# Fewer weight tiles decoded beside the attention pairs, one PSUM layout for all stages, and the transposes of the exponentials one pair later

## The chip, the core and the metric

The kernel runs on one core of one Trainium2 chip. The metric is the device time of one execution in microseconds (us), as a median of several runs. A core has a matrix engine (PE, which also loads the stationary operand, PEld), a vector engine (DVE), a scalar engine (ACT), a third elementwise engine (POOL), and a queue that issues DMAs (SP). Each runs its own list of instructions in order; semaphores tie them to each other.

## What is computed

Three blocks follow each other: causal attention with a memory term, a feed-forward block with the gate h * tanh(softplus(h)), and a second block that multiplies two projections.

```python
scores = scale * np.matmul(q, k.transpose(0, 1, 3, 2))      # B, H, S, D = 4, 8, 576, 64
scores = np.where(causal, -1000000000.0, scores)
a = np.exp(scores - scores.max(-1, keepdims=True))
local = np.matmul(a / (a.sum(-1, keepdims=True) + 1e-09), v)
q_p = phi(q)                                                 # x > 0: x + 1, else exp(x)
mem_out = einsum(q_p, M_prev) / (einsum(q_p, z_prev) + 1e-06)
x = g * mem_out + (1 - g) * local                            # 2304 rows, 512 columns
h = x @ w_in                                                 # 512 to 2048
x2 = (h * np.tanh(softplus(h))) @ w_out                      # 2048 to 512
out = ((x2 @ w1) * (x2 @ w2)) @ w3 @ w_out2                  # 512 to 1024, 1024, 512
```

All weights come as 64-bit floats, so the kernel has to make 32-bit words of them itself.

## The kernel before

**Tiles to decode.** A weight tile of 128 rows and 512 columns arrives as 512 KB of pairs of 32-bit words. `decode` (lines 104 to 133) turns it into fp32: six operations on DVE (lines 114, 116, 118, 121, 125 and 127) and one addition on POOL (line 132). `to_split` (lines 149 to 154) then writes two parts, `hi` and `lo`, with two more operations on POOL (lines 77 and 80); `to_dram` does the same and sends the result to DRAM for later. A decoder has a number of raw buffers and of working buffers: beside the attention one of each, in the middle stage three and two.

**The attention** goes over 16 pairs of heads, one turn p of the loop at line 521 for each pair, and a 17th turn, the drain. In a turn PE makes the scores of four row blocks (`s_blocks`) and of the last 64 rows (`s_last`). DVE adds the mask and takes the maximum (line 374), ACT takes the exponential with its sum (line 379), and `normed` (lines 358 to 371) multiplies the exponentials by the inverse sums: DVE takes five blocks, POOL four (line 369 both). PE then transposes the exponentials in seven groups (`pt_g`, lines 422 to 432): group 1 and group 0 hold blocks of the pair's first head, 2 and 3 of the second, 4 blocks of both, 5 and 6 the last rows. ACT copies each group out of its PSUM bank (line 431). `pv` multiplies them by v, after a product of `phi` with the memory matrix; `prep` and `trans_phi` transpose q, k and phi for the next pair, through the two banks called X. `in_turn` ties each of these pieces behind PE's last instruction, so the order of PE is the order of the calls; the rest is put in order by a scheduler.

In turn p groups 4, 2, 3, 5 and 6 of pair p - 1 are transposed among the scores of pair p. Groups 1 and 0 of pair p come at the end of the same turn p, behind `pv` of pair p - 1. A tile is decoded in each of the turns 2 to 11: eight of the first quarter of the weights (`lq0`: four of w_in, four of w_out) and two of those for later (`pre`). The scheduler puts each about a turn earlier.

**The middle stage** has 24 units (g, n): a quarter g of the hidden columns and a chunk n of 384 rows. `emit_h` makes four products h of 128 columns and passes them through tanh, arctan and sine on ACT. DVE multiplies the result `y` by h (line 493); this last reading of h frees its PSUM bank. `split_y` splits the product, `emit_x2` multiplies it by w_out and DVE adds it to x2 (line 610). On PE a unit is 48 matmuls of h and 48 of x2 of the unit before. Two tiles are decoded beside nearly every unit of g = 0 to 2. In g = 3 `fold` multiplies w3 by w_out2 on PE beside the units, 16 tiles of w3.

**PSUM** has eight banks. The attention takes two pairs A, two X and two F. At the end of the drain this pool is closed and another opened, with A 3, X 3 and F 2 as single banks: `emit_h` takes A, A, F, F (in g = 3 A, A, A, X), `emit_x2` X. The last stage (`emit_ab`, `emit_out`) takes A and F for its two products and X, X, X, F for its output.

## Time and profile before

| | us |
|---|---|
| median of 3 runs | 1037.8 |
| lowest and highest run | 1034.76 and 1038.8 |
| the profiled execution | 1035.9 |
| its span, first to last instruction | 1034.1 |
| attention, first score to the last `pv` but one | 8.6 to 261.7 |
| drain, to the first matmul of `emit_x2` | 261.7 to 293.4 |
| middle stage, g = 0 to 2 | 293.4 to about 580 |
| g = 3 with `fold`, and the change to the last stage | about 580 to 780 |
| last stage | 780 to 1034 |

The profile is read from a trace of one execution. It has busy times by engine, windows (busy time of each engine in a stretch, with the clock that was granted to PE as a share of 2.4 GHz), waits (which engine sat idle, and whose event ended that) and timelines. PE is busy for 95% of the span; what is to be found is where the other engines set PE's pace.

### The profile page before, as it was taken

To read this page: it belongs to the slowest core of one execution; us is meant where nothing else is said; L and a number is where in the kernel's file an instruction comes from. 1 tells how busy PE (TensorE), PEld (TensorE's weight loads), DVE (VectorE), ACT (ScalarE), POOL (GpSimd) and SP (SyncE) were. 2 spreads that over 40 slices of the span, in tenths; PEclk is the share of its full clock that TensorE was granted. 3 is DMA by queue.
4 is the path that set the end of the run, shared out by engine and by line. 5 is a ranking of instruction groups with operands and counts; after the bars stand their busy time and mean duration, and the time that the engine had idled before them with its cause. 6 is when DMAs were issued, how large, how long until landed. Compare 5 with 4: busy or idle time off the path is not lost.

```text
span 1034.1 us, 15144 instructions
## 1 busy us (share of the span) xinstructions
PE 979.9 (95%) x5584; PEld 830.1 (80%) x5584; DVE 602.9 (58%) x1364; ACT 506.9 (49%) x1016; POOL 336.2 (33%) x345
## 2 busy tenths in 40 slices
PE   5888888999899999999999999999989999999998
PEld 3445455565699999999999999999768888888897
DVE  4888988675377666757575676668973121121111
ACT  4676767888646565565656545443323121221212
POOL 6676666552155334352524221112550000000000
PEclk8998999999999999999999999999999999999999
DMA  7343434320143133112312356222410010100101
GB/s 157 93 114 93 96 93 122 91 52 14 61 143 102 46 117 106 59 61 103 123 41 82 137 193 226 91 78 82 152 41 1 1 41 1 41 1 1 41 1 61
DMA packets 93626, 81.73 MB, mean 79 GB/s; under 512 B 68720, under 2 KB 72816, under 8 KB 93552
## 3 DMA queue, kind: packets, MB, share of 16 engines
q1 hardware_dynamic: 92224, 80.44, 25.2%
q8 instruction: 44, 0.72, 0.3%
q10 hardware_dynamic: 1328, 0.33, 0.2%
q14 instruction: 30, 0.25, 0.1%
HBM read 65.54 MB, written 15.20 MB: 78 GB/s over the span
## 4 chain that ended last, share of the span: by engine, by line
PE 73%; DVE 13%; ACT 7%; POOL 2%; issue 2%; DMA 2%; SPq 0%; ACTq 0%; DVEq 0%; POOLq 0%
PE psX L64 30%; PE psA L64 24%; PE psF L64 17%; ACT s L379 3%; DVE s L374 2%; DVE s L369 2%; PE psF L67 1%; DVE da L118 1%; DVE phie L333 1%; ACT pt L431 1%; POOL s L369 1%; DVE da L114 1%; DVE xt L80 1%; DVE draw L127 1%; PE psF L634 1%
## 5 line engine op out<-in xcount | busy, mean ns | idle before, releaser
L132 POOL TENSOR_TENSOR da<-da,draw 128x512 f32<-128x512 f32 x72 | 104.8, 1464 | 333.6 <-DVE draw L127 253.3
L64 PE MATMUL psX<-gh,wqt 128*128 128x384 f32 x768 | 196.1, 335 | 0.0
L64 PEld LDWEIGHTS psX<-gh,wqt 128*128 128x128 f32 x768 | 138.8, 188 | 1.0 <-DVE y L493 0.3
L64 PE MATMUL psX<-gl,wqt 128*128 128x384 f32 x384 | 128.2, 335 | 0.0
L64 PE MATMUL psA<-xt,wqt 128*128 128x384 f32 x648 | 118.9, 335 | 0.0
L64 PEld LDWEIGHTS psA<-xt,wqt 128*128 128x128 f32 x648 | 112.8, 188 | 0.7 <-DVE s L369 0.2
L379 ACT ACTIVATE s<-s,acc 128x512 f32<-128x512 f32 (+2 forms) x144 | 83.7, 587 | 19.1 <-DVE acc L374 18.4
L67 PEld LDWEIGHTS psF<-ident,s 128*128 128x128 f32 x400 | 44.7, 144 | 55.2 <-ACT pt L431 13.3
L67 PE MATMUL psF<-ident,s 128*128 128x128 f32 x400 | 67.1, 294 | 19.8 <-DVE xt L80 8.0
L64 PE MATMUL psA<-x2h,w12t 128*128 128x512 f32 (+1 forms) x288 | 80.7, 355 | 4.2 <-POOL w12t L77 3.6
L64 PE MATMUL psX<-wft,room 128*128 128x512 f32 x336 | 82.6, 390 | 0.0
L431 ACT COPY pt<-psF 128x512 f32<-128x512 f32 (+1 forms) x112 | 56.9, 538 | 44.8 <-PE psF L67 42.2
L64 PE MATMUL psF<-xt,wqt 128*128 128x384 f32 x408 | 75.2, 339 | 2.8 <-DVE xt L80 2.8
L753 ACT COPY bs<-psA 128x512 f32<-128x512 f32 (+1 forms) x40 | 21.8, 545 | 114.2 <-PE psA L64 106.2
L64 PEld LDWEIGHTS psF<-xt,wqt 128*128 128x128 f32 x408 | 72.4, 191 | 2.9 <-DVE xt L80 2.9
L64 PEld LDWEIGHTS psX<-wft,room 128*128 128x128 f32 x336 | 62.6, 188 | 12.7
L64 PEld LDWEIGHTS psX<-gl,wqt 128*128 128x128 f32 x384 | 72.1, 188 | 0.3
L610 DVE TENSOR_TENSOR x<-x,psX 128x384 f32<-128x384 f32 x72 | 39.6, 549 | 53.7 <-PE psX L64 53.5
L374 DVE CUSTOM_DVE_ANT_0 s<-psA,mask 128x512 f32<-128x512 f32 (+2 forms) x144 | 62.7, 477 | 9.2 <-PE psA L64 9.2
L64 PE MATMUL psA<-x2s,w12t 128*128 128x512 f32 x288 | 67.9, 389 | 0.0
L501 ACT CAST gh<-y 128x768 fp32r<-128x768 f32 x48 | 40.1, 837 | 55.5 <-PE psX L64 53.4
L755 ACT CAST room<-bs 128x512 fp32r<-128x512 f32 (+1 forms) x40 | 23.1, 578 | 84.9 <-DVE bs L754 84.7
(123 smaller groups left out, 1896.2 us busy)
## 6 DMA issues: line engine op xcount, KB each, us to landing
draw<-in_moe_w_dram SPq DMA_DIRECT2D x32, 512.0 KB, 3.7
draw<-in_moe_w_out_dram SPq DMA_DIRECT2D x24, 512.0 KB, 3.8
draw<-in_moe_w_in_dram SPq DMA_DIRECT2D x16, 512.0 KB, 4.0
out_dram<-ob SPq DMA_DIRECT2D x18, 256.0 KB, 2.0
raw<-in_q_dram SPq DMA_DIRECT2D x32, 128.0 KB, 3.2
raw<-in_v_dram SPq DMA_DIRECT2D x32, 128.0 KB, 2.7
o_dram<-draw SPq DMA_DIRECT2D x8, 512.0 KB, 2.8
w_dram<-draw SPq DMA_DIRECT2D x8, 512.0 KB, 2.8
```

The costliest lines, as they stand in the source:

```text
L64: tail[0] = nc.tensor.matmul(o, lhsT=l, rhs=r, start=start, stop=stop).ins
L67: tail[0] = nc.tensor.transpose(o, src, ident).ins
L80: return (eng or nc.vector).tensor_tensor(out=dst, in0=src, in1=f(hi), op=ALU.subtract)
L132: nc.gpsimd.tensor_tensor(out=a, in0=a, in1=lw.bitcast(F32), op=ALU.add)
L369: (nc.gpsimd if x in ON_POOL else nc.vector).tensor_scalar(out=s, in0=s, scalar1=d["sum"][:, x:x + 1], scalar2=og[:, x:x + 1], op0=ALU.mul ...
L374: nc.vector.tensor_tensor_reduce(out=s, in0=o, in1=m, op0=ALU.add, op1=ALU.min, scale=-scale, scalar=init, accum_out=a,)
L379: nc.scalar.activation(out=s, in_=s, func=AF.Exp, scale=-1.0, bias=a, accum_out=r)
L431: nc.scalar.copy(out=t[:, 0:n], in_=o[:, 0:n])
L501: nc.scalar.copy(out=gh, in_=y[i])
L610: r = nc.vector.tensor_tensor(out=d, in0=d, in1=o, op=ALU.add)
L753: nc.scalar.copy(out=bs, in_=pb)
L755: nc.scalar.copy(out=t[:, 0, 0:n], in_=bs)
```

## The change

Three things change together.

First, the order of the attention. Groups 1 and 0 of pair p - 1 move from the end of turn p - 1 to turn p, behind the first scores of pair p, and the groups 4, 2 and 3 move a place later each. `prep` of k moves ahead of groups 5 and 6, `s_last` ahead of `normed`. The transposed groups get six buffers of 512 columns and one of 128, in place of five.

Second, the tiles. Beside the pairs only four are decoded, the w_in tiles of `lq0` (turns 3, 6, 9 and 12), each with one buffer as before. The four w_out tiles are decoded in the drain with a decoder of two raw and two working buffers. All 16 tiles of `pre` go to the middle stage, where four units, (1, 0), (1, 2), (2, 0) and (2, 2), take a third tile.

Third, PSUM. One pool serves all stages: two pairs A, two X, two F. `emit_h` takes two pairs for its four products; `emit_x2` takes X, F, X, F, and X alone in g = 3; `emit_ab` takes a pair, `emit_out` X, F, X, F. In the drain `emit_h` of unit (0, 0) comes first, and that of unit (0, 1) is called there too, behind `pv` of the last pair.

```diff
-    sk = ExitStack()
-    pool = [sk.enter_context(tc.tile_pool(name="ps0", bufs=1, space=PSUM))]
-    banks = {"X": 2, "F": 2}
+    ps = ctx.enter_context(tc.tile_pool(name="ps", bufs=1, space=PSUM))
 
     def bank(tag):
-        return pool[0].tile([128, 512], F32, tag=tag, name="ps" + tag, bufs=banks[tag])
+        return ps.tile([128, 512], F32, tag=tag, name="ps" + tag, bufs=2)
 
     def psA():
-        return pool[0].tile([128, 2, 512], F32, tag="A", name="psA", bufs=2)
+        return ps.tile([128, 2, 512], F32, tag="A", name="psA", bufs=2)
...
     def in_turn(fn, *args):
 
-        if tail[0] is None:
+        if not ordered[0]:
             return fn(*args)
...
     def pt_g(p, gi):
         d = st[p]
-        t = ap_.tile([128, 512], F32, tag="pt", name="pt", bufs=5)
+        n = 128 * len(GROUPS[gi])
+        t = ap_.tile([128, n], F32, tag=f"pt{n}", name="pt", bufs=6 if n == 512 else 1)
         o = psF()
-        n = 128 * len(GROUPS[gi])
...
-    HT = ("AAFF", "AAAX")
-    HU = {(0, 1): "FXFX"}
...
         for m in range(KQ):
-            if u == (0, 0):
-                if m % 2 == 0:
-                    two = psA()
-                o = two[:, m % 2, 0:CH]
-            else:
-                o = bank(HU.get(u, HT[g == NQ - 1])[m])[:, 0:CH]
+            if m % 2 == 0:
+                two = psA()
+            o = two[:, m % 2, 0:CH]
...
-    background = chain(lq0, pre)
     for p in range(NPAIR + 1):
 
         now, old, new = p < NPAIR, p > 0, p + 1 < NPAIR
+        ordered[0] = 1 <= p < NPAIR
...
+            lk = ExitStack()
+            decoder(lk, 2, 2, side="right")
...
         if now:
             in_turn(s_blocks, p, (3,))
+        else:
+            split = split_y((0, 0), emit_h((0, 0)))
         if old:
-            in_turn(pt_g, p - 1, 4)
-            in_turn(pt_g, p - 1, 2)
+            in_turn(pt_g, p - 1, 1)
+            in_turn(pt_g, p - 1, 0)
+        if not now:
+            run(lq0, 2)
+            run(lq0, 2)
         if now:
             in_turn(s_blocks, p, (2,))
...
         if old:
-            in_turn(pt_g, p - 1, 3)
+            in_turn(pt_g, p - 1, 4)
+            in_turn(pt_g, p - 1, 2)
         if new:
             in_turn(prep, p + 1, "q")
+        if old:
+            in_turn(pt_g, p - 1, 3)
         if now:
             in_turn(s_blocks, p, (0, 1))
-        if not now:
-            run(lq0, 100)
+        if new:
+            in_turn(prep, p + 1, "k")
         if old:
             in_turn(pt_g, p - 1, 5)
-            if not now:
-                split = split_y((0, 0), emit_h((0, 0)))
             in_turn(pt_g, p - 1, 6)
         if now:
+            in_turn(s_last, p)
             normed(p, [(i, e) for e in range(2) for i in range(4)])
-        if new:
-            in_turn(prep, p + 1, "k")
-        if 2 <= p < 12:
-            run(background, 1)
-        if now:
-            in_turn(s_last, p)
         if p == 0:
             in_turn(trans_phi, 0)
+        if p in (3, 6, 9, 12):
+            run(lq0, 1)
         if old:
             in_turn(pv, p - 1)
-        if now:
-            in_turn(pt_g, p, 1)
+        if not now:
+            early = {(0, 1): emit_h((0, 1))}
         if new:
             prep_phi(p + 1)
-        if now:
-            in_turn(pt_g, p, 0)
-        if new:
             in_turn(trans_phi, p + 1)
...
-    sk.close()
-    pool[0] = ctx.enter_context(tc.tile_pool(name="ps", bufs=1, space=PSUM))
-    banks.update(A=3, X=3)
...
-            o = psX()[:, 0:CH]
+            o = bank("X" if g == NQ - 1 else "XF"[m % 2])[:, 0:CH]
...
         with tc.issue_after(split):
-            if u == (0, 0):
-                run(pre, 2)
-            if n == 0:
+            if n == 0 and not last:
                 run(pre, 2)
             elif not last:
                 run(nextq if n < 4 else chain(islice(nextq, 1), islice(pre, 1)), 2)
+            if g in (1, 2) and n in (0, 2):
+                run(pre, 1)
...
-        pb, pa = (bank(t)[:, 0:n] for t in ("AA", "AF")[m % 2])
+        pair = psA()
+        pb, pa = pair[:, 0, 0:n], pair[:, 1, 0:n]
...
-            outs[c] = [bank(tag) for tag in "XXXF"[0:n // 128]]
+            outs[c] = [bank(tag) for tag in "XFXF"[0:n // 128]]
```

What this makes of PE's list, at the end of a turn. `psF` is a bank of F, `s0` to `s3` are the exponentials of row blocks 0 to 3, `phie` is phi of the next pair, `kt,qt` the first scores of the next pair. Before:

```order
L64 MATMUL psF_2858<-phi_2533,mr1_110 64x64 x2
L64 MATMUL psF_2858<-pt_2820,raw_2150 64x64 x8
L64 MATMUL psF_2858<-pt_2827,raw_2150 64x64 x2
L67 MATMUL psF_2885<-ident_66,s1_2814 128x128
L67 MATMUL psF_2885<-ident_66,s2_2776 128x128
L67 MATMUL psF_2885<-ident_66,s3_2753 128x128 x2
L67 MATMUL psF_2905<-ident_66,s0_2808 128x128
L67 MATMUL psF_2905<-ident_66,s1_2814 128x128
L67 MATMUL psF_2905<-ident_66,s2_2776 128x128
L67 MATMUL psF_2905<-ident_66,s3_2753 128x128
L67 MATMUL psX_2912<-ident_66,phie_2891 128x128 x2
L67 MATMUL psX_2916<-ident_66,phie_2891 128x128 x3
```

After:

```order
L63 MATMUL psF_2784<-phi_2433,mr1_110 64x64 x2
L63 MATMUL psF_2784<-pt_2756,raw_2076 64x64 x8
L63 MATMUL psF_2784<-pt_2763,raw_2076 64x64 x2
L66 MATMUL psX_2824<-ident_66,phie_2810 128x128 x2
L66 MATMUL psX_2828<-ident_66,phie_2810 128x128 x3
L63 MATMUL psA_2836<-kt_2746,qt_2708 128x512 x2
L66 MATMUL psF_2846<-ident_66,s1_2740 128x128
L66 MATMUL psF_2846<-ident_66,s2_2688 128x128
L66 MATMUL psF_2846<-ident_66,s3_2665 128x128 x2
L66 MATMUL psF_2853<-ident_66,s0_2734 128x128
L66 MATMUL psF_2853<-ident_66,s1_2740 128x128
```

The two groups of transposes stood ahead of phi's and of the next scores; now they stand behind both, and phi's transposes follow straight on the last matmuls of `pv`.

PE's list where the drain begins; `xt` is x, so `psA<-xt,wqt` is `emit_h` of unit (0, 0). Before:

```order
L64 MATMUL psX<-pt,raw 64x256 x2
L64 MATMUL psX<-pt,raw 64x128 x2
L64 MATMUL psA<-xt_81,wqt 128x384 x14
L64 MATMUL psF<-phi,mr_110 64x64 x2
L64 MATMUL psF<-pt,raw 64x64 x10
L67 MATMUL psF<-ident,s_3148 128x128
L67 MATMUL psF<-ident,s_3124 128x128
L67 MATMUL psF<-ident,s_3101 128x128 x2
L64 MATMUL psA<-xt_81,wqt 128x384 x20
L67 MATMUL psF<-ident,s_3142 128x128
```

After:

```order
L63 MATMUL psX<-pt,raw 64x128 x2
L63 MATMUL psX<-phi,mr_110 128x512
L63 MATMUL psA<-xt_81,wqt 128x384 x3
L63 MATMUL psF<-phi,mr_110 64x64 x2
L63 MATMUL psF<-pt,raw 64x64 x10
L63 MATMUL psA<-xt_81,wqt 128x384 x45
L66 MATMUL psF<-ident,s_3074 128x128
L66 MATMUL psF<-ident,s_3036 128x128
```

`emit_h` was cut into pieces between the transposes; now all its 48 matmuls stand ahead of them.

PE's list where the drain ends, from the last product of `pv`; `gh` is the split product, so `psX<-gh` is the first of `emit_x2`. Before:

```order
L64 MATMUL psX<-pt,raw 64x128 x2
L64 MATMUL psF<-phi,mr_110 64x64 x2
L64 MATMUL psF<-pt,raw 64x64 x10
L64 MATMUL psF<-xt_81,wqt 128x384 x12
L64 MATMUL psX<-xt_81,wqt 128x384 x12
L64 MATMUL psF<-xt_81,wqt 128x384 x12
L64 MATMUL psX<-xt_81,wqt 128x384 x12
L64 MATMUL psX<-gh,wqt 128x384 x2
```

After:

```order
L63 MATMUL psX<-pt,raw 64x128 x2
L63 MATMUL psA<-xt_81,wqt 128x384 x14
L63 MATMUL psF<-phi,mr_110 64x64 x2
L63 MATMUL psF<-pt,raw 64x64 x10
L63 MATMUL psA<-xt_81,wqt 128x384 x34
L63 MATMUL psX<-gh,wqt 128x384 x2
L63 MATMUL psX<-gl,wqt 128x384
L63 MATMUL psX<-gh,wqt 128x384 x2
```

`emit_h` of unit (0, 1) took single banks F and X behind `pv`; now it takes the pairs A, and its first 14 matmuls stand ahead of the short product of `pv`.

On DVE the third tile of such a unit is interleaved with the unit's own operations; its first stands ahead of the second pair's product with `y`. In the drain ten operations of the third and fourth w_out tile stand ahead of the first product with `y` of unit (0, 0).

In g = 3 the order of PE moves too: of the 16 sets of transposes of `fold` 4 stood behind the last matmul of `emit_h`, and now 6.

## Rows read from the trace of the kernel before

**Rows 1.** The page: busy time of engines, share of the span, instructions.

```profile
PE 979.9 (95%) x5584; PEld 830.1 (80%) x5584; DVE 602.9 (58%) x1364; ACT 506.9 (49%) x1016; POOL 336.2 (33%) x345
```

**Rows 2.** Windows: stretch, length, busy us (instructions) of PE, PEld, DVE, ACT, POOL, PE's clock, DMA.

```profile
8.58:27.18 18.60, 13.28 (x49) 7.62 (x49) 11.86 (x40) 9.95 (x29) 11.32 (x14) 0.73 0.68 150
27.18:196.80 169.62, 143.95 (x1021) 85.95 (x1020) 144.20 (x414) 118.63 (x339) 111.93 (x124) 0.96 0.40 102
196.80:238.73 41.93, 39.14 (x307) 24.64 (x306) 29.15 (x105) 35.78 (x103) 21.95 (x26) 1.00 0.24 55
45.25:63.51 18.26, 14.94 (x103) 8.66 (x102) 15.25 (x43) 11.76 (x34) 11.94 (x14) 0.93 0.37 95
181.74:196.80 15.06, 13.56 (x103) 8.21 (x102) 10.82 (x35) 11.92 (x35) 9.98 (x12) 1.00 0.38 98
```

**Rows 3.** Waits of PE from 45 to 182 us: who, for whom, us, times, longest.

```profile
PE psF L67 <- DVE xt L80: 6.6, 6, 2.1
PE psF L67 <- POOL s L369: 4.0, 6, 0.9
...
PE psF L67 <- DVE s L369: 1.3, 3, 0.8
```

**Rows 4.** Waits of PE from 196.8 to 252 us.

```profile
PE psX L64 <- ACT kt L309: 2.0, 3, 0.7
PE psF L67 <- DVE xt L80: 1.0, 4, 0.3
```

**Rows 5.** Timeline of PE, first turn: start, us, line, what, idle before.

```profile
23.58 0.47 PE L67 MATMUL psF<-ident,s 128*128 128x128 f32 x1 [1.07 <-DVE s L369]
```

**Rows 6.** Timeline of PE from the last turn through the drain.

```profile
258.44 1.02 PE L64 MATMUL psX<-phi,mr 128*128 128x512 f32 x2
...
279.84 0.34 PE L64 MATMUL psF<-phi,mr 128*64 128x64 f32 x4 [1.79 <-ACT pt L431]
...
283.55 3.78 PE L64 MATMUL psF<-xt,wqt 128*128 128x384 f32 x12 [2.79 <-DVE xt L80]
287.17 2.24 PE L64 MATMUL psX<-xt,wqt 128*128 128x384 f32 x12
...
293.41 0.51 PE L64 MATMUL psX<-gh,wqt 128*128 128x384 f32 x2
```

**Rows 7.** Timeline of ACT in the drain: table load, arctan.

```profile
274.52 1.28 ACT L486 ACT_TABLE_LOAD   x1
...
275.92 1.75 ACT L489 ACTIVATE y<-y,half 128x768 f32<-128x768 f32 x2
```

**Rows 8.** The page: DMAs of w_out tiles, us to landing.

```profile
draw<-in_moe_w_out_dram SPq DMA_DIRECT2D x24, 512.0 KB, 3.8
```

**Rows 9.** Timeline of DVE and POOL in a middle unit: two tiles, products.

```profile
403.98 0.79 DVE L114 TENSOR_SCALAR da<-draw 128x512 int32<-128x512 int32 x2
...
407.90 1.29 DVE L127 SCALAR_TENSOR_TENSOR draw<-draw 128x512 f32<-128x512 uint32 x2
...
414.62 1.02 DVE L493 TENSOR_TENSOR y<-y,psA 128x384 f32<-128x384 f32 x2 [1.89 <-ACT y L491]
...
408.72 2.87 POOL L132 TENSOR_TENSOR da<-da,draw 128x512 f32<-128x512 f32 x2 [10.10 <-DVE draw L127]
...
412.73 2.56 POOL L80 TENSOR_TENSOR wqt<-da,wqt 128x512 fp32r<-128x512 f32 x2
```

**Rows 10.** Timeline of PE: `emit_h` of the next unit begins.

```profile
418.21 4.32 PE L64 MATMUL psA<-xt,wqt 128*128 128x384 f32 x24
```

**Rows 11.** Windows: the first group of unit (0, 1), and one middle unit.

```profile
283.55:287.17 3.62, 3.62 (x12) 3.62 (x13) 3.62 (x10) 1.28 (x1) 0.00 (x0) 0.56 0.00 0
...
418.21:434.85 16.64, 16.64 (x97) 16.64 (x97) 10.82 (x22) 9.73 (x13) 6.57 (x6) 1.00 0.20 64
```

**Rows 12.** Timeline of DVE: `normed` of a turn with a tile, and without.

```profile
143.79 2.53 DVE L369 TENSOR_SCALAR s<-s,sum,ogp 128x256 f32<-128x256 f32 x4
...
260.68 1.45 DVE L369 TENSOR_SCALAR s<-s,sum,ogp 128x256 f32<-128x256 f32 x4
```

More of the change, by code (lines that the diff above doesn't have):

```diff
@@ L61, in fused_kernel @@
     tail = [None]
+    ordered = [False]
     def mm(o, l, r, start, stop):
@@ L96, in fused_kernel, with decoder @@
     dec = {}
-    def decoder(stack, raw, n, w=WN):
-        dec.update(pool=stack.enter_context(tc.tile_pool(name="dec", bufs=1)), raw=raw, n=n, w=w)
+    def decoder(stack, raw, n, w=WN, side="left"):
+        dec.update(pool=stack.enter_context(tc.tile_pool(name="dec", bufs=1, side=side)), raw=raw, n=n, w=w)
     def dec_tile(tag):
@@ L576, in fused_kernel @@
             normed(p, [(4, None)])
+    lk.close()
     at.close()
-    sk.close()
-    pool[0] = ctx.enter_context(tc.tile_pool(name="ps", bufs=1, space=PSUM))
-    banks.update(A=3, X=3)
     w2q[0] = ctx.enter_context(tc.tile_pool(name="w2q", bufs=1))
@@ L684, in fused_kernel @@
                 decoder(fk, 2, 2)
-            y = emit_h(u, folding if last and n > 0 else iter(()))
+            y = early.pop(u) if u in early else emit_h(u, folding if last and n > 0 else iter(()))
         if last and n == 3:
```

## Prediction

> **What bounds the kernel now.** I read the busy times first: PE 979.9 of 1034.1 us, DVE 602.9, POOL 336.2 [rows 1]. PE is short of its share only in the attention and the drain, so the second view is the windows there, cut at the first scores of each pair. Turns 1 to 10, each with a decoded tile, last 169.62 us, 16.96 each; turns 11 to 13, with none, 41.93 us, 13.98 each [rows 2]. Without a tile PE is busy 39.14 of 41.93 us and ACT 35.78: PE nearly sets the pace. With a tile PE is busy 143.95 of 169.62, at a granted clock of 0.96, and DVE as long, 144.20. The excess is 29.8 us over ten tiles, 2.98 each. The third view, the waits of PE, says where half of it goes: in turns 2 to 9 the transposes of exponentials waited 6.6 us for DVE's subtraction from `pv`'s bank, 4.0 us for POOL's part of `normed` and 1.3 us for DVE's [rows 3], 11.9 us in eight turns, 1.49 each. In four turns without a tile it was 1.0 us, 0.25 each [rows 4]. Last, the middle stage: a unit of 16.64 us has PE busy all of it, DVE 10.82 us [rows 11].
>
> **The change, part by part.** The sum is made against the profiled execution, 1035.9 us, which is 1.9 below the median of 1037.8 and inside the runs' range; the forecast is for a median near its fellow.
>
> *Six tiles fewer beside pairs.* At 2.98 us each: -17.9. It is right if the excess belongs to the tiles. The bounds are single turns: the last, where only a tile's end on POOL is left, is 15.06 us, 1.08 over a free one; turn 2 is 18.26, 4.28 over [rows 2]. Six of these give -6.5 and -25.7. I take the mean, since turns 1 to 10 all carry a tile and nothing else sets them apart as a group from turns 11 to 13.
>
> *Groups 1 and 0 a turn later.* Between `pv` and these groups now lie phi's transposes and the next first scores, and they read exponentials that POOL and DVE normalised a while ago. Four turns keep a tile; each loses the wait of 1.49 us down to the 0.25 of a free one: -5.0. The other end is 0, if DVE and POOL make PE wait at the next place instead, for DVE is as busy as PE in such turns. In the first turn the wait of 1.07 us goes [rows 5]: -1.1.
>
> *Free turns.* Nothing leaves PE's list here, only its order. What could be gained is PE's idle time, (41.93 - 39.14) / 3 = 0.93 us a turn. What could be lost: phi's transposes now follow `pv` directly, and their second half needs the bank X that ACT's copy and DVE's subtraction have to free first; groups 4, 2 and 3 need copies that ACT makes behind two exponentials of the new pair. Both engines have some room (ACT 85% busy), and the wait for k's copy, 2.0 us in four turns [rows 4], shrinks as k is prepared earlier. I take 0 for about 13 turns, ends -12 (all the idle time) and +10 (0.8 a turn).
>
> *The drain.* From the last but one `pv` at 258.44 to the first matmul of `emit_x2` at 293.41 are 34.97 us. PE's long idle times in it are 1.79 and 2.79 us, and the first group after the second took 3.6 us (to 287.17) where its neighbour takes 2.1 [rows 6]: 6.1 us that are no work at full clock. The last wait goes, with its slow group (4.3 us), since unit (0, 1) takes pairs that are already there. But `emit_h` no longer fills the gaps between the transposes. With two banks F, the third pair of groups waits for a copy that stands on ACT behind a table load, 1.28 us, and two arctans, 1.75 [rows 7]: some 3.2 us with the copy ahead, and by the same count about 1 us for group 6. That is all but given back: -1.0. The w_out tiles do not end last if they run as in the middle: issue at 258.44 at the earliest, landing 3.8 us [rows 8], 5.2 us of DVE for two (403.98 to 409.19), 1.4 on POOL, then landing and DVE again (9.0), then 6.6 us on POOL (408.72 to 415.29) [rows 9]: near 285, or 288 with DVE's other work; `emit_x2` comes at about 292. If they are later, `emit_x2` waits, and so does unit (0, 1), for ten operations of tiles three and four stand on DVE ahead of the product that frees its banks. Ends: -5 and +4.
>
> One rule bears on this. Four DVE operations of `normed` took 2.53 us in a turn with a tile, and 1.45 in the last turn, though POOL works beside both [rows 12]: a POOL operation can hold DVE up, and need not. The Trainium skill (SBUF — State Buffer, "Who interferes with whom") states it harder: DVE and GpSimd share a port pair under an exclusive lock, and the second to come blocks fully. By that rule the POOL operations on the tiles in the drain, 13 us, of which about 9 lie beside DVE's work, would be added to DVE's time; `emit_x2` would start near 297, 4 us later than now, and the sum be 1017. The rows agree only in part, and I keep the rows' case.
>
> *Tiles moved to the middle.* Two more there, and four units with a third tile: 2.6 us of DVE [rows 9] into 5.8 us that DVE has free in a unit (16.64 - 10.82). Cost 0; without that cover, 2.6 each, 10 at most.
>
> *PSUM.* A pair is free when DVE has multiplied both halves. That is at 414.62 + 1.02 = 415.64, and the next `emit_h` starts at 418.21 [rows 9, 10]: 2.57 us to spare where before a third bank A made the first product independent of it. So 0. With four banks in place of three, `emit_x2` can't be worse in g = 0 to 2. In g = 3 it has two X. There two more tiles of w3 stand behind the last `emit_h`, 5.2 us of DVE in a stretch where DVE also decodes the last eight tiles; but that `emit_h` comes earlier by the matmuls which now follow it. I take +1.5, ends 0 and +5.2. The last stage has four banks for products and four for outputs in either layout: 0.
>
> Sum: -17.9 - 5.0 - 1.1 + 0 - 1.0 + 0 + 1.5 = -23.5, so 1035.9 - 23.5 = 1012.4.
>
> **The rivals.**
> *A. The excess is not the tiles'.* The early turns run at lower clock (0.73 in the first turn, 0.96 over turns 1 to 10 [rows 2]) and with more DMA, and would stay long without a tile; or free turns get longer by the waits named. For it: turns 1 to 10 shorten towards the end, from 18.26 to 15.06, with a tile in all of them. Against it: the drop from 15.06 to 13.98 comes exactly where the tiles end. With -6.5 in place of -17.9 it gives 1024.
>
> *B. PE's own work becomes the limit.* Free turns fall to PE's busy time of 13.05 us and turns with a tile follow: -23.5 - 10 gives 1002. For it: phi's transposes and scores now fill the very gap in which PE waited. Against it: ACT, 85% busy, has to follow.
>
> *C. Slower: the paired banks.* The product with `y` comes later than the next `emit_h`, so PE idles in each of 22 units. The price is not only the wait: after 2.79 us of idle time [rows 6] PE ran its next group at a granted clock of 0.56, close to the lower level of 1.2 GHz, in 3.62 us in place of 2.1 [rows 11]. At 1.0 us of waiting and 1.5 of slow clock a unit, 22 units cost 55, less 23.5: 1067. It decides from the point where DVE's product slips by more than the 2.57 us to spare. Against it: DVE's order around `y` is the same as before in all but four units. The Trainium skill (TensorE: Matmul & The Clock Gate, "A second HAM failure mode: psum-queue depth-cycling") describes this case, short idle times between groups from cycling through banks, paid by the clock. No row of the middle stage shows it so far, its clock being 1.00.
>
> *D. The change does not do what it says.* A scheduler sets all but PE's order in the attention. The lists show the new order in place, so I leave this nothing.
>
> **How the numbers follow.** Forecast, 1006 to 1021: 0.63. A, 1021 to 1032: 0.17. B, 995 to 1006: 0.12. C, above 1043: 0.05. No difference: 0.03. The range leaves out C and the ends of A and B: 1000 to 1028. A measurement of this kernel can tell about 0.5%, 5.2 us, from no change; A's best part and the forecast lie below 1032.6. Faster 0.91, same 0.04, slower 0.05.
>
> **What would show it.** Right: windows cut at the first scores give about 14 us for turns without a tile and 15.5 to 16.5 for the four with one; the waits of transposes for `normed` and for the subtraction from `pv`'s bank are gone from the attention; the drain is 33 to 35 us with its gap ahead of the third pair of groups; the middle unit stays at 16.64 us at clock 1.00; the last stage is unchanged. Wrong: free turns over 14.5 us (A), or at 13.1 (B); idle time of PE before `emit_h` for DVE's `y`, and a clock under 1.00 in the middle (C); more idle time of PE than now between the fold and the last stage.

## The result and the profile after

The changed kernel takes **1025.05 us** (median of 4 runs, 1024.33 to 1025.24), the kernel before 1036.41 us beside it; the ratio is 0.989, with a 95% interval of 0.986 to 0.991. So it is faster, but by 11.4 us and not by the 23.5 of the prediction's sum. The time lies inside the range.

The profiled execution has a span of 1023.2 us where that of before had 1034.1. Its page, as in [rows 1]:

```profile
PE 977.8 (96%) x5584; PEld 829.1 (81%) x5584; DVE 612.0 (60%) x1364; ACT 500.7 (49%) x1016; POOL 339.0 (33%) x345
```

PE's busy time has hardly moved; what went is idle time. Cut at the same matmuls as the prediction (first scores of a pair, `pv` of the last pair but one, first matmul of `emit_x2`), the 10.9 us lie like this:

| stretch | before | after | difference | predicted |
|---|---|---|---|---|
| start to the last `pv` but one | 258.44 | 243.11 | -15.3 | -24.0 |
| drain | 34.97 | 34.26 | -0.7 | -1.0 |
| `emit_x2` of (0, 0) to `emit_h` of (3, 0) | 274.6 | 275.5 | +0.9 | 0 |
| g = 3, fold and last stage, to the end | 466.1 | 470.4 | +4.2 | +1.5 |

The drain is counted from the last `pv` but one, at 258.44 before; the 261.7 that the table of times ahead of the prediction gives for it is where `emit_h` begins.

The windows of the attention after (columns as in [rows 2]: start:end, length, busy us of PE, PEld, DVE, ACT and POOL, PE's granted clock, DMA). Rows 1 to 5 are turns 0 to 4, the sixth is the seven turns 5 to 11, and the last is g = 1 of the middle stage:

```profile
8.57:24.06 15.49, 8.93 (x39) 4.93 (x39) 9.83 (x39) 8.77 (x27) 9.63 (x12) 0.92 0.71 160
24.06:44.23 20.17, 15.42 (x103) 9.59 (x102) 17.99 (x46) 11.75 (x35) 14.76 (x16) 0.84 0.49 122
44.23:61.43 17.20, 15.28 (x104) 9.38 (x103) 14.67 (x41) 11.93 (x34) 11.96 (x15) 0.86 0.35 88
61.43:76.78 15.35, 14.57 (x104) 9.16 (x103) 12.11 (x39) 11.93 (x34) 10.79 (x12) 0.89 0.37 95
76.78:95.27 18.49, 14.91 (x104) 9.65 (x103) 14.03 (x45) 12.02 (x34) 12.15 (x14) 0.91 0.26 59
95.27:192.89 97.62, 92.68 (x716) 57.71 (x715) 67.75 (x246) 82.02 (x238) 52.04 (x63) 1.00 0.35 78
...
352.25:452.56 100.31, 100.21 (x577) 99.79 (x577) 80.61 (x144) 57.04 (x78) 47.05 (x42) 1.00 0.30 102
```

All four tiles beside pairs are decoded in turns 1 to 4: the code calls them at p = 3, 6, 9 and 12, but nothing holds them there, and DVE, POOL and the queues take them as soon as the one buffer is free. These turns take 71.2 us together where the same turns of before, which also held a tile each, took 70.4. Free turns take 13.95 us, as forecast, against 13.98 before. Turn 0 falls by 3.1 us, and turn 14 with the stretch behind it grows by 2.6, since two groups moved on by a turn. So the whole gain in the attention is turns that have no tile any more.

What PE waits for in turn 1 (columns: who, line, for whom; us in total, times, longest):

```profile
PE psX L66 <- DVE xt L79: 4.4, 1, 4.4
```

and in turn 4:

```profile
PE psF L66 <- ACT pt L430: 2.0, 1, 2.0
PE psF L66 <- DVE xt L79: 1.2, 1, 1.2
```

The waits for `normed` [rows 3] are gone (one for the subtraction is left, 1.2 us in turn 4), and another has come in their place: line 66 into bank X is the second half of phi's transposes. PE in turn 1 (start, us, line, what, idle time before and who ended it):

```profile
38.52 0.44 PE L66 MATMUL psX<-ident,phie 128*128 128x128 f32 x2
43.40 0.90 PE L66 MATMUL psX<-ident,phie 128*128 128x128 f32 x3 [4.43 <-DVE xt L79]
```

and DVE at that time:

```profile
39.07 1.03 DVE L341 TENSOR_TENSOR dn<-dn,gates 128x10 f32<-128x10 f32 x1
...
40.45 2.23 DVE L368 TENSOR_SCALAR s<-s,sum,ogp 128x256 f32<-128x256 f32 x4
...
42.66 0.68 DVE L79 TENSOR_TENSOR xt<-psX,xt 128x512 fp32r<-128x512 f32 x1
```

After `pv` the second half needs the bank that DVE's subtraction `xt<-psX` frees. That subtraction stands on DVE behind four operations of `normed`, which stand behind a tile's operations and phi's. PE stands still for 4.43 us. The price is paid twice here, for the granted clock falls as well. Three windows behind waits of 4.43, 1.82 and 1.22 + 2.02 us:

```profile
43.40:47.00 3.60, 3.60 (x11) 1.76 (x12) 2.09 (x7) 1.06 (x2) 2.45 (x4) 0.50 0.35 79
...
62.00:65.00 3.00, 3.00 (x14) 1.98 (x12) 2.46 (x6) 1.73 (x4) 1.72 (x2) 0.60 0.06 12
86.00:89.00 3.00, 3.00 (x16) 2.58 (x13) 1.20 (x8) 3.00 (x13) 3.00 (x4) 0.59 0.51 116
```

The clock there is 0.50 to 0.60: PE runs all or most of these windows at the lower level, 1.2 GHz. The first 3 us of turn 1 are at 0.50 too, behind a wait of 3.50 us in turn 0. Of the 15.4 us by which turns 1 to 4 exceed four free turns, 8.1 are idle time of PE (11.0 against 0.72 a free turn) and 7.3 are slow matmuls (PE busy 60.2 us against 4 x 13.23).

The drain went as forecast: one short gap and one of 1.98 us ahead of the third pair of groups, then `emit_x2` without a wait:

```profile
258.31 1.15 PE L66 MATMUL psF<-ident,s 128*128 128x128 f32 x8 [0.57 <-ACT pt L430]
...
262.44 1.14 PE L66 MATMUL psF<-ident,s 128*128 128x128 f32 x8 [1.98 <-ACT pt L430]
...
277.37 0.51 PE L63 MATMUL psX<-gh,wqt 128*128 128x384 f32 x2
```

From the fold to the end PE waits more than before: 8.4 us in place of 5.5 (3.6 for POOL's decoded tile, 1.2 in the fold, 0.7 for ACT's copy). Most of it is now for DVE's product of a tile in the last stage, and for POOL's decoded tile:

```profile
PE psA L63 <- DVE bs L749: 4.6, 3, 3.0
PE psA L63 <- POOL w12t L76: 2.1, 3, 1.5
```

The timeline of ACT shows why the longest of them, 3.05 us, is so long. The casts of the next columns (`x2s`) stand ahead of tile 4's copy and wait 16.91 us for POOL's last decoded tile (the decoder's space is closed for them, `fk.close()`); the copy, DVE's product and the bank pair queue up behind them:

```profile
746.28 0.62 ACT L750 CAST room<-bs 128x512 fp32r<-128x512 f32 x1
763.81 2.18 ACT L731 CAST x2s<-x 128x512 fp32r<-128x512 f32 x4 [16.91 <-POOL w12t L79]
765.89 0.57 ACT L748 COPY bs<-psA 128x512 f32<-128x512 f32 x1
```

PE at the end of that wait:

```profile
767.61 0.50 PE L63 MATMUL psA<-x2h,w12t 128*128 128x512 f32 x1 [3.05 <-DVE bs L749]
```

### The profile page after: what moved, and what is told of

Same layout as the page of the kernel before. It is cut to its first block, busy times and chain, and to the rows that moved or that the text cites. A ratio compares the mean times of both kernels' runs of the same rounds, so it can differ in the third digit from the quotient of the medians.

```text
span 1023.2 us, 15086 instructions
## 1 busy us (share of the span) xinstructions
PE 977.8 (96%) x5584; PEld 829.1 (81%) x5584; DVE 612.0 (60%) x1364; ACT 500.7 (49%) x1016; POOL 339.0 (33%) x345
## 4 chain that ended last, share of the span: by engine, by line
PE 71%; DVE 12%; ACT 11%; DMA 2%; POOL 2%; issue 2%; SPq 0%; POOLq 0%; ACTq 0%; DVEq 0%
PE psA L63 37%; PE psX L63 16%; PE psF L63 14%; ACT s L378 5%; ACT pt L430 3%; DVE s L368 2%; PE psF L66 2%; DMA draw<-in_moe_w_dram 1%; DVE da L120 1%; PE psX L66 1%; DVE xt L79 1%; POOL da L131 1%; DVE draw L126 1%; DVE da L117 1%; DVE s L373 1%
## 5 line engine op out<-in xcount | busy, mean ns | idle before, releaser
L63 PE MATMUL psA<-xt,wqt 128*128 128x384 f32 x1152 | 207.5, 335 | 0.2
L63 PEld LDWEIGHTS psA<-xt,wqt 128*128 128x128 f32 x1152 | 200.0, 188 | 2.4 <-DVE y L487 0.8
L63 PE MATMUL psX<-gh,wqt 128*128 128x384 f32 x480 | 122.4, 335 | 1.1 <-DVE x L604 1.1
L63 PEld LDWEIGHTS psX<-gh,wqt 128*128 128x128 f32 x480 | 86.9, 188 | 2.3 <-DVE x L604 1.4
L63 PEld LDWEIGHTS psA<-x2h,w12t 128*128 128x128 f32 x384 | 68.3, 189 | 20.7 <-DVE bs L749 5.0
L63 PEld LDWEIGHTS psA<-x2s,w12t 128*128 128x128 f32 x384 | 72.1, 188 | 14.9
L373 DVE CUSTOM_DVE_ANT_0 s<-psA,mask 128x512 f32<-128x512 f32 (+2 forms) x144 | 63.4, 483 | 34.4 <-PE psA L63 34.3
L63 PE MATMUL psF<-gh,wqt 128*128 128x384 f32 x288 | 73.1, 334 | 0.0
L487 DVE TENSOR_TENSOR y<-y,psA 128x384 f32<-128x384 f32 x96 | 48.7, 549 | 34.9 <-ACT y L485 34.9
L63 PE MATMUL psA<-room,w12t 128*128 128x512 f32 (+1 forms) x192 | 68.0, 354 | 0.0
L368 POOL TENSOR_SCALAR s<-s,sum,ogp 128x128 f32<-128x128 f32 (+1 forms) x64 | 53.1, 840 | 37.2 <-DVE sum L364 37.2
```

The lines of the kernel that those rows point to most:

```text
L63: tail[0] = nc.tensor.matmul(o, lhsT=l, rhs=r, start=start, stop=stop).ins
L368: (nc.gpsimd if x in ON_POOL else nc.vector).tensor_scalar(out=s, in0=s, scalar1=d["sum"][:, x:x + 1], scalar2=og[:, x:x + 1], op0=ALU.mul ...
L373: nc.vector.tensor_tensor_reduce(out=s, in0=o, in1=m, op0=ALU.add, op1=ALU.min, scale=-scale, scalar=init, accum_out=a,)
L487: nc.vector.tensor_tensor(out=y[i][:, j], in0=y[i][:, j], in1=hp[2 * i + j], op=ALU.mult)
```

## The experiments

The times of a run stand beside the kernel before on the same chip. "Rest" is the span from the first `emit_x2` to the end; among the five profiles that have the changed kernel's code there, and its drain, it is 745.6 to 749.5 us, so only differences above 4 us mean anything in that column. (With the old place of groups 1 and 0, half of `emit_h` of unit (0, 1), 24 matmuls, comes behind the first `emit_x2` and counts as rest and not as drain.) The attention of the changed kernel's code is 242.8 to 244.3 us in four profiles.

| kernel | median us | ratio to before, 95% | to last `pv` but one | drain | rest |
|---|---|---|---|---|---|
| before | 1036.41 | 1 | 258.4 | 35.0 | 740.7 |
| changed | 1025.05 | 0.986 to 0.991 | 243.1 | 34.3 | 745.8 |
| four tiles, old order | 1044.03 | 1.004 to 1.008 | 242.7 | 36.1 | 762.3 |
| late tiles, old order | 1034.66 | 0.995 to 0.999 | 235.7 | 35.1 | 761.2 |
| late tiles | 1020.29 | 0.982 to 0.986 | 237.1 | 34.3 | 745.6 |
| adjacent late tiles | 1020.68 | 0.982 to 0.986 | 237.3 | 33.1 | 749.4 |
| phi in bank F | 1015.80 | 0.978 to 0.981 | 232.2 | 34.1 | 747.6 |
| late tiles, phi in F | 1011.30 | 0.971 to 0.976 | 226.9 | 34.2 | 749.5 |
| old place of groups 1 and 0 | 1042.50 | 1.002 to 1.006 | 260.3 | 28.4 | 753.5 |
| ACT's order | 1023.43 | 0.983 to 0.988 | 242.8 | 34.2 | 743.7 |
| halves of pairs | 1025.82 | 0.987 to 0.991 | 244.3 | 34.2 | 747.8 |
| single banks, last stage | 1033.94 | 0.995 to 0.998 | 243.3 | 34.2 | 755.6 |
| single banks, everywhere | 1027.34 | 0.988 to 0.993 | 249.6 | 32.7 | 745.7 |
| late, phi in F, ACT's order | 1006.73 | 0.969 to 0.972 | 226.8 | 34.1 | 743.9 |
| the same, single banks | 1004.38 | 0.966 to 0.972 | 226.7 | 32.7 | 742.5 |

### Fewer tiles alone, or the order: four tiles in the old order

```diff
-        if 2 <= p < 12:
+        if p in (3, 6, 9, 12):
             run(background, 1)
...
-            run(lq0, 100)
+            with tc.issue_after(held[0]):
+                run(lq0, 100)
```

`held[0]` is DVE's last subtraction of the `pv` before; the line keeps the other four tiles out of the attention.

> The kernel before with four tiles beside pairs in place of ten, at the places where the changed kernel's fall (turns 1 to 4), the other four of the first quarter held back to the drain, which grows; order and banks are those of before. The attention up to the last pv but one, 258.4 us before, is what is compared. The prediction's step (2.98 us a tile, wherever): six turns at 14.0 us, attention 240 to 242. Rival from the run with late tiles (a tile costs 1.6 us in a settled turn of the new order, an early turn without one 2.4 more than a free turn): turns 5 to 10 fall from 99.2 to between 84 and 90 us, turns 1 to 4 stay at 70: attention 243 to 249. The new order can then have gained 0 to 6 us in the attention.

Windows of turns 1 to 4 and of turns 5 to 10:

```profile
26.91:96.14 69.23, 56.93 (x409) 35.38 (x409) 59.13 (x167) 47.11 (x135) 46.65 (x52) 0.95 0.42 102
96.14:181.05 84.91, 78.50 (x613) 49.27 (x612) 59.51 (x210) 71.54 (x205) 44.90 (x54) 1.00 0.34 77
```

Turns 5 to 10 take 84.9 us in place of 99.2, 2.4 us for each tile that went, and turns 1 to 4 take 69.2. The attention is 15.75 us shorter than before. The changed kernel's is 15.33 us shorter. Within the 1.5 us by which profiles of one code differ, **the new order has gained nothing in the attention**; fewer tiles have gained all of it. With the old order the groups wait in turns 1 to 4 as they did:

```profile
PE psF L67 <- DVE xt L80: 4.6, 3, 2.1
...
PE psF L67 <- POOL s L369: 2.0, 3, 1.0
PE psF L67 <- DVE s L369: 2.0, 2, 1.0
```

These are 8.6 us. In the same turns of the changed kernel phi's second half waits 6.6 us for the subtraction, and the groups 2.0 for ACT's copy and 1.2 for the subtraction: 9.8 us.

And yet this kernel is slower than before: the rest costs 21.6 us more. PE waits 17.4 us there in place of 5.5, and its busy time is 9.5 us longer. The tiles that were taken out of the turns are late behind the drain, first POOL's tile of the first quarter (waits of PE from 278 to 700 us):

```profile
PE psX L64 <- POOL wqt L77: 3.2, 1, 3.2
```

later ACT's casts in the last stage (from 700 us on):

```profile
PE psX L64 <- ACT room L758: 2.8, 1, 2.8
PE psX L64 <- ACT wft L789: 2.7, 1, 2.7
```

The tiles' place is all that the edit changes; how the waits of the last stage come from it was not followed. So the change's other parts (the drain's order and its two-tile decoding, third tiles in the middle, banks) are what lets the gain through: with them the rest costs 5.1 us more than before in place of 21.6. Which of them does how much was not tried.

### The order with settled tiles: old and new

The same kernel in the old order with the four tiles held to turns 3, 6, 9 and 12 (`with tc.issue_after(held[0]):` ahead of `run(background, 1)`), and the changed kernel with its tiles held to the same turns:

```diff
         if p in (3, 6, 9, 12):
-            run(lq0, 1)
+            with tc.issue_after(held[0]):
+                run(lq0, 1)
```

> The kernel before with four tiles beside pairs, held to turns 3, 6, 9 and 12, the other four of the first quarter in the drain; only the attention up to the last pv but one is compared, with 237.1 us for the same tiles in the new order. If the new order takes 1.24 us off each turn with a tile (the prediction's step): turns 3, 6, 9 and 12 at 16.5 to 17 us in the old order and the attention 242 to 244. If it is worth nothing: 15.4 to 15.9 us a turn, attention 236 to 239.

> The four tiles decoded beside pairs are held on DVE behind the subtraction of the pv before, so that they lie in turns 3, 6, 9 and 12; in the changed kernel they lie in turns 1 to 4, which take 20.2, 17.2, 15.4 and 18.5 us where free turns take 13.95. Theory 'tiles': the excess of 15.4 us belongs to the tiles and goes with them, so turns 1, 2, 4 and 5 fall to 14 to 14.5 us, turns 3, 6, 9 and 12 rise to 15.5 to 18, and the time stays within 4 us of 1025. Rival 'early turns' (rival A of the prediction): turns 1, 2 and 4 stay above 16.5 us without a tile, and the late tiles cost under 1 us each: time 1022 to 1029. Third possibility, 'both together': a tile is dear only where the pipeline is still settling; turns 1, 2, 4 and 5 fall under 14.5 and turns 3, 6, 9 and 12 stay under 15.5 us: time 1013 to 1018.

Windows of turns 3 (with a tile) and 4, old order:

```profile
57.95:72.76 14.81, 13.57 (x104) 8.21 (x103) 12.07 (x39) 11.94 (x35) 10.98 (x12) 1.00 0.44 106
72.76:86.73 13.97, 13.04 (x103) 8.21 (x103) 9.75 (x35) 11.92 (x35) 7.59 (x9) 1.00 0.34 77
```

and of turns 1, 2 and 3 (the last with a tile), new order:

```profile
24.61:40.91 16.30, 14.06 (x104) 8.46 (x103) 12.85 (x40) 11.83 (x35) 13.35 (x15) 0.96 0.49 116
40.91:54.85 13.94, 13.24 (x104) 8.25 (x103) 9.57 (x35) 11.72 (x34) 7.00 (x10) 1.00 0.25 57
54.85:70.39 15.54, 13.22 (x104) 8.26 (x103) 13.34 (x42) 11.82 (x34) 10.83 (x13) 1.00 0.44 110
```

In the new order turns 2 and 4 fall to 13.95 us without a tile, and turn 1 keeps 16.3: only the first turns are long by themselves, turn 1 by 2.4 us (3.0 in the next run). A tile then costs 1.6 us (15.54 in turn 3), all of it idle time at clock 1.00, in two waits:

```profile
PE psF L66 <- ACT pt L430: 1.3, 1, 1.3
PE psX L66 <- DVE xt L79: 0.9, 1, 0.9
```

In the old order the same tile costs 0.83 us (14.81), and the attention is 1.3 us shorter. So the new order makes a turn with a tile dearer, by some 0.8 us, where the prediction had taken 1.24 off. One reason can be seen: the subtraction that the tile is held behind ends earlier there, so the tile begins 1.3 us ahead of its turn (56.68), beside groups 1 and 0. How much of the 0.8 us that is was not tried. And in the old order no wait for `normed` is left in such a turn. Of PE's two waits in turn 3 of the old order the first, 0.7 us, is for k's copy, and the second is:

```profile
PE psF L67 <- DVE xt L80: 0.5, 1, 0.5
```

My own expectation for the old order, 15.4 at the least, was too high as well.

### Early, or adjacent

The four tiles held to turns 9 to 12, one behind the other:

```diff
-        if p in (3, 6, 9, 12):
+        if p in (9, 10, 11, 12):
```

> The four tiles held to four turns in a row, 9 to 12, late and in a settled pipeline. In turns 1 to 4 of the changed kernel they cost 3.9 us each, of which PE's idle time is about half and slow matmuls (granted clock 0.84 to 0.91) the other; each apart in turns 3, 6, 9 and 12 they cost 1.6 us at clock 1.00. If adjacency is what makes them dear: turns 9 to 12 take 16.5 to 19 us at a clock under 0.95, and the time is 1023 to 1026. If the early turns are: 15.4 to 15.7 us each at clock 1.00, time 1019 to 1021, as with the tiles apart.

Turn 10 and the free turn 13:

```profile
154.25:169.84 15.59, 13.22 (x103) 8.27 (x102) 13.39 (x42) 11.81 (x34) 10.83 (x13) 1.00 0.41 104
...
201.01:214.95 13.94, 13.23 (x103) 8.24 (x102) 9.66 (x36) 11.71 (x34) 6.82 (x9) 1.00 0.07 17
```

The four turns take 15.42, 15.59, 15.59 and 15.58 us at clock 1.00. Being adjacent costs nothing in the new order. What made the tiles dear is that they lay in turns 1 to 4, or that nothing held them to a place within a turn; no run held tiles in turns 1 to 4, so these two are not told apart. Holding them later takes 5.8 to 6.0 us off the attention, somewhat less than the slow matmuls of turns 1 to 4 were (7.3).

### The new wait: phi's second half in another bank

```diff
-            pt = psX()
+            pt = psX() if c0 == 0 else second()
...
-        trans(st[p]["e"], lambda cs, o: nc.scalar.copy(out=t[:, cs], in_=o))
+        trans(st[p]["e"], lambda cs, o: nc.scalar.copy(out=t[:, cs], in_=o), psF)
```

> The second half of phi's transposes goes into a bank F instead of the bank X that pv has just filled, so it no longer waits for DVE's subtraction; nothing else changes. Theory: this wait, 10.1 us in the whole of the changed kernel (4.4 of them in turn 1, 1.8 in turn 2, 0.3 in most others), is what the new order put in place of the waits for normed; it goes and PE gains most of it: turn 1 at 15 to 17 us, turn 2 at 15 to 16, free turns at 13.6 to 13.7, time 1014 to 1020. Rival: DVE is late anyway and the next reader of its work (the first copies of groups, or the scores' banks) waits instead: turn 1 stays above 18.5 us, time 1022 to 1026.

Windows of turns 2 and 3 (each with a tile) and of a free turn:

```profile
37.44:55.21 17.77, 14.80 (x104) 9.72 (x103) 16.64 (x48) 13.35 (x39) 14.14 (x16) 0.90 0.38 90
55.21:74.78 19.57, 16.17 (x103) 9.89 (x102) 16.61 (x48) 12.07 (x35) 15.32 (x17) 0.83 0.42 108
116.71:130.09 13.38, 13.02 (x104) 8.27 (x103) 9.67 (x37) 11.67 (x35) 7.55 (x10) 1.00 0.36 81
```

The wait is gone everywhere. Free turns fall from 13.95 to 13.38 us, turn 1 from 20.2 to 15.0, and the attention from 243.1 to 232.2. Turns 2 and 3 do not follow: 17.8 and 19.6 us at clock 0.90 and 0.83, since PE waits there for `normed` (3.0 us in turn 2) and for ACT's copies (2.9 in turn 3). With the late tiles as well:

> Both edits that helped: the four tiles held to turns 3, 6, 9 and 12, and phi's second half in a bank F. If they add up (attention of 243.1 us shorter by 6.0 and 11.0, less what both count in turns 1 to 4): free turns 13.4, turns with a tile 14.5 to 15, turn 1 at 14 to 15, attention 222 to 228, time 1004 to 1011. If the two have one cause and don't add: 1014 to 1017, with turns of over 15.5 us where a tile lies.

The two nearly add up, 226.9 us to the last `pv` but one. Turns 2 to 13 take 167.4 us where twelve free ones would take 160.6: 1.7 us a tile again.

### Only groups 1 and 0 back

```diff
-        if old:
-            in_turn(pt_g, p - 1, 1)
-            in_turn(pt_g, p - 1, 0)
...
+        if now:
+            in_turn(pt_g, p, 1)
         if new:
             prep_phi(p + 1)
+        if now:
+            in_turn(pt_g, p, 0)
+        if new:
             in_turn(trans_phi, p + 1)
```

> Only the order of groups 1 and 0 goes back to that of before (behind pv, around phi's preparation); four tiles beside pairs, the drain and the banks stay as changed. By the prediction's step the new order is worth 6 us (1.24 in each of four turns with a tile, 1.1 in the first): time 1030 to 1032, waits of these groups for normed back at about 1.5 us in each turn with a tile. Theory now: the new order trades them for the wait of phi's transposes and is worth little in turns with a tile: turns 1 to 4 together within 3 us of 71.2, free turns within 0.1 of 13.95, time 1022 to 1028; in the first turn the order gains 3 us.

Here the two groups alone went back behind `pv`, the rest of the new order staying. This was a bad undoing: free turns rise to 15.27 us, and four of the nine to between 16.3 and 16.7, at a lower clock. With groups 1 and 0 gone from the start of the turn, groups 4 and 2 and then 3 follow so close on each other that group 3 waits for a copy on ACT. PE in turn 7:

```profile
132.19 0.71 PE L66 MATMUL psX<-ident,raw 128*128 128x128 f32 x5
134.66 0.66 PE L66 MATMUL psF<-ident,s 128*128 128x128 f32 x4 [1.75 <-ACT pt L430]
```

It does not tell what the order of before was worth (the runs above do). It shows only that this part of the new order can't be taken back by itself.

### The last stage

ACT's casts of `x2s` held behind the copy of tile 5 (`emit_ab` returns its copy):

```diff
-        emit_ab(k)
+        done = emit_ab(k)
...
-            split_x2(c + 1)
+            with tc.issue_after(done):
+                split_x2(c + 1)
```

> In the last stage the casts of the next columns of x2 (x2s) are held behind ACT's copy of the product of tile 5; in the changed kernel they stand ahead of tile 4's copy and wait 16.9 us for POOL's last decoded tile, and PE then waits 3.05 us for tile 4's product. Theory: ACT's queue is what the 3.05 us are; they go with about 1 us of slow matmuls, and the 1.5 us for POOL's tile stay: time 1021 to 1022, first matmul on x2s 3 to 4.5 us earlier against the start of the stage. Rival: DVE is late by its own list (tiles and casts), the product comes no earlier, or the casts now come too late for their first matmul: the same time within 1 us.

Waits of PE in the last stage with this edit:

```profile
PE psA L63 <- DVE bs L749: 2.7, 3, 1.2
```

The waits for the product are 2.7 us, here and in the other run with this edit, where they are 4.6 in five of six runs with pairs and without this edit (3.5 in the other, the late tiles). The time is 1.6 us shorter, and 4.6 us on top of the two edits above. Neither is clear of noise, for the intervals overlap each time, and in the second pair of profiles part of it is the clock (last section). The pairing was tried in three ways. First, two pairs taken once, their halves used in turn:

```diff
+    pairs = [psA(), psA()]
...
-        pair = psA()
+        pair = pairs[k % 2]
```

> In the last stage the two pairs of banks A are taken once and their halves used in turn, so that the first product of a tile needs only ACT's copy and not DVE's product to be through; the order on each engine is the same. Theory: the pairing is what costs 4.6 us of waiting for DVE's product in the last stage, where before only 0.7 us were waited for its copy; about half of it goes (1.1 us at 746, 0.4 at 738, and about 1 of the 3.05 us at 767), with its slow matmuls: 2 to 4 us, time 1021 to 1023. Rival: PE waits at the second product instead, or for POOL's tiles of w1 and w2: the same time within 1 us.

This run says nothing on its question: taken as halves of two lasting pairs, the first product's matmuls still waited for DVE, 4.6 us again. Second, the banks opened anew for the last stage, four of them single:

```diff
+    sk.close()
+    ps[0] = ctx.enter_context(tc.tile_pool(name="ps", bufs=1, space=PSUM))
...
-        pair = psA()
-        pb, pa = pair[:, 0, 0:n], pair[:, 1, 0:n]
+        pb, pa = bank("B")[:, 0:n], bank("B")[:, 0:n]
```

> The last stage opens its banks anew: four single banks for the products in place of two pairs, as many as before, each free as soon as its one reader is through; attention and middle stay as changed. Theory: with singles the waits for DVE's product shrink from 4.6 us to 1 to 2, as in the kernel before (0.7 us), while the opening of the banks costs up to 1 us at the start of the stage: 1022 to 1024. Rival: the waits are DVE's and ACT's lateness and come back in front of the next product, 3 us or more: 1025 to 1027.

Waits of PE there:

```profile
PE psB L64 <- ACT wo L644: 6.1, 1, 6.1
...
PE psB L64 <- DVE bs L749: 1.3, 2, 1.0
```

With single banks the waits for the product shrink to 1.3 us, but opening the banks waits 6.1 us for the fold's last output. Third, single banks in the whole kernel:

```diff
     def psA():
-        return ps.tile([128, 2, 512], F32, tag="A", name="psA", bufs=2)
+        return bank("A"), bank("A")
```

> The changed kernel with four single banks A in place of two pairs, in all stages, so each bank is free when its own reader is through; nothing else is edited. If the pairing is what the last stage lost: its waits for DVE's product shrink from 4.6 us to 1 to 2.5, and with the slow matmuls behind them the time is 1021 to 1023. The middle stage gives nothing (no wait there); the attention gives 0 to 2 us, in the wait for the maxima of 2.7 us in the first turn. If the pairing costs nothing and DVE is late by its own list: 1024 to 1026, the waits standing ahead of the second product.

Waits of PE in the last stage:

```profile
PE psA L63 <- POOL w12t L76: 5.0, 3, 3.6
PE psA L63 <- DVE bs L749: 1.2, 1, 1.2
```

Nothing has to be opened anew here. The product waits 1.2 us in place of 4.6, and POOL's decoded tile 5.0 in place of 2.1. The rest is 745.7 us, as with pairs. So **no cost of the pairing shows there**: what one wait gives up, the wait for POOL's tile takes. In the attention single banks lose 6.5 us (free turns 14.36), with another order of PE's matmuls; together with late tiles and phi in F they lose nothing there (226.7 us against 226.8).

### A version that beats both

> Three edits together: the four tiles apart in turns 3, 6, 9 and 12, phi's second half in a bank F, and the casts of the last stage behind the copy of tile 5. With the first two the time was 1011.3; the third gave 1.6 to 2.5 us alone and touches another stage, so if it adds: 1008 to 1010. If the wait of 1.5 us for POOL's tile takes over: 1010 to 1012.

> The same three edits and single banks A in all stages. If single banks help where pairs wait: 1006 to 1009. If the waits are DVE's lateness: as without them, 1008 to 1011; over 1012 if the other order of the scores' matmuls that it allows disturbs the copies of groups.

Late tiles, phi in F and ACT's order together take 1006.73 us, and with single banks 1004.38, a ratio of 0.969 (0.966 to 0.972) to before. The intervals of these two overlap.

## Why the prediction was wrong, point by point

*Six tiles fewer, -17.9.* Right in its place, a little too large: alone they gave 15.75 us. But the price of a tile is no constant. It was 2.4 us in turns 5 to 10 of before, 0.83 in a settled turn of the old order with free turns around it, 1.6 in the new, and 3.9 in turns 1 to 4 of the changed kernel, where turn 1 alone has 2.4 us without a tile. The mean over ten turns that all had a tile could not show that.

*Groups 1 and 0 a turn later, -5.0 and -1.1.* **This is the step that failed.** The waits for `normed` went, as it said, but others took their place. The prediction asked what was late next only in general ("if DVE and POOL make PE wait at the next place instead") and took the end without that. The next place had been named, one paragraph on, under free turns: phi's second half needs the bank that DVE's subtraction frees. In a free turn that is 0.3 us. In a turn with a tile the subtraction stands behind `normed` and the tile, and the wait was 0.9 us in a settled turn and 4.4 in turn 1; the wait for ACT's copies grew as well, from 0.3 us in a free turn to 1.3 in a settled turn with a tile. With the tiles in turns 1 to 4, 8.6 us of waiting became 9.8. With settled tiles there was little to save: the 1.49 us a turn were read where every turn has a tile, and in the old order 0.5 us for the subtraction is all that is left of them in a turn with a tile. With phi in F, where that wait is gone, PE waits 3.0 us for `normed` again in turn 2. In sum the new order gave +0.4 us with the tiles early, which is nothing within the spread of profiles, and +1.3 with the tiles late, in place of -6.1. Turn 0 did fall by 3.1 us, but since two groups of transposes moved from it into turn 1; PE's idle time in it grew, from 5.3 to 6.6 us.

*Where the tiles lie.* The prediction gave them 15.5 to 16.5 us each, which is what they cost in turns 3, 6, 9 and 12 (15.4 to 15.6). They were not there. That they lay in turns 1 to 4, held to no place there, and that the gaps also cost the clock, made 6 us more.

*Free turns, 0.* Right: 13.95 us.

*The drain, -1.0.* Right in sum (-0.7) and in the place of its gap, with some luck: the terms given, 6.1 or 4.3 us gained and 4.2 paid, make -1.9 or -0.1, and the gap was 1.98 us and not 3.2, with none at group 6. The w_out tiles did not end last. The Trainium skill (SBUF — State Buffer, "Who interferes with whom") was weighed there without the conditions that the section sets (a DVE operation in a two-port mode, or one with two inputs in SBUF against a POOL operation that reads SBUF). That would have put `emit_x2` 4 us later; it came 0.7 us earlier. What it states for two inputs is seen in the turns, though (last section).

*Tiles moved to the middle, 0.* Nearly: units with a third tile keep 16.64 us, the last three units of g = 1 and 2 grow by 0.07 to 0.27. Rival C fell with that: the clock is 1.00 throughout.

*PSUM and transition, +1.5.* Measured +4.2, inside its ends; but the last stage, taken at 0, has most of it. Some 2 us are ACT's casts standing ahead of a copy. What the other 2 are is not settled, and they are near what two profiles differ by. No run shows the pairing to be the cause.

*The rivals.* Rival A had the time nearly (1024), by luck: its sum has -6.5 for the tiles and -6.1 for the order, and the runs show -15.75 and about 0. Of its mechanism the first turns hold in part: turn 1 is long without a tile, turn 2 is not; what was dear is a tile, held to no place, in an early turn. Rival B's faster free turns did not come by themselves: it took the bank F for phi to get from 13.95 to 13.38.

## What to carry to other kernels

When a wait is taken from an engine, follow the engine that it waited for: what that one still has to do first decides where the next wait stands, and a bank that must be freed by the same late engine gives the whole gain back. Where two parts of a change save the same wait, count it once: with free turns around it, a tile left the new order no wait for `normed` to save. Look up where a scheduler puts work that nothing holds, and hold it where gaps are cheap. And work taken out of a crowded stage needs a place: the same six tiles gave 15.75 us in the attention and lost 21.6 behind it until the later stages were made for them.

## What was not expected of the hardware

A gap in PE's work is sometimes paid twice, and its length does not tell when. Behind waits of 4.43 and 1.82 us in turns 1 and 2 the granted clock was 0.50 and 0.60; behind one of 1.84 us in turn 1 of the run with late tiles it was 1.00. The last stage has the same wait of 3.05 us in each of the five profiles that the column "rest" compares. The 3 us behind it in the changed kernel, and with late tiles and phi in F:

```profile
767.61:770.61 3.00, 3.00 (x13) 2.50 (x14) 1.38 (x2) 1.43 (x3) 0.00 (x0) 1.00 0.02 5
...
752.15:755.15 3.00, 3.00 (x7) 2.42 (x8) 1.38 (x2) 1.43 (x3) 0.00 (x0) 0.50 0.02 5
```

PE does 13 matmuls in the first and 7 in the second. The clock fell behind it in the three profiles with a rest of 747.6 to 749.5 us, and not in the two with 745.6 and 745.8, so this is much of the spread in that column. With groups 1 and 0 in their old place a wait of 1.75 us stands in each of the turns 5 to 13, and behind four of the nine the clock fell. What decides it no run here shows. In turns 1 to 4 it made nearly half of the excess: 7.3 of 15.4 us are slow matmuls. The prediction had this price for rival C only, and not for the turns with a tile.

A POOL operation holds DVE up to its very end, but not every DVE operation. The product `dn<-dn,gates`, ten elements a row with both inputs in SBUF, took 0.16 to 0.17 us the twelve times that POOL was idle at that moment. The four times that POOL was at work it lasted until POOL's operation ended. Turn 1, with POOL's addition of a tile (38.79 + 1.28 = 40.07; 39.07 + 1.03 = 40.10; DVE's row stands above). POOL:

```profile
38.79 1.28 POOL L131 TENSOR_TENSOR da<-da,draw 128x512 f32<-128x512 f32 x1 [0.62 <-DVE draw L126]
```

DVE, where POOL was idle, in turn 8:

```profile
142.78 0.17 DVE L341 TENSOR_TENSOR dn<-dn,gates 128x10 f32<-128x10 f32 x1
```

Earlier in turn 1 it took 1.51 us beside a product of POOL that ended with it (31.45 + 1.65 = 33.10; 31.61 + 1.51 = 33.12). Four operations of `normed`, with one input, took 2.23 us in turn 1 and 1.45 in turn 4, POOL at work beside both. The Trainium skill (SBUF — State Buffer, "Who interferes with whom") says that a DVE operation with two inputs in SBUF contends with a POOL operation that reads SBUF; the trace agrees, at up to 1.35 us an operation (1.51 - 0.16). It agrees in the whole changed kernel: of the decoder's operations with two inputs in SBUF (lines 120 and 126) 19 began while POOL was at work, and each took 0.30 to 1.02 us longer than the shortest of its line; of the products with h and the additions to x2 (lines 487 and 604), whose second input is in PSUM, 65 did, and none took more than 0.01 us longer. So a tile's operations on POOL cost DVE time too, 0.87 us of it in turn 1 (1.03 - 0.16), and that is a part of why the subtraction came late.
